# Staging the queries of a slot with one POOL copy in place of four, in a two-part decode attention kernel

## The chip, the cores and the metric

The kernel runs on one core of a Trainium2 chip. The metric is the device time of one execution in microseconds (us). For a program on one core, an execution counts as slow when it lies more than 1.5% above the fastest of the same kernel; all comparisons here use fast runs.

Engines: PE (matrix), DVE (VectorE), ACT (ScalarE), POOL (GpSimd), SP (SyncE, which issues the large loads and the output here). "Span" is the time from the first to the last instruction in the profile. In the profiled execution of the kernel before it is 1.8 us shorter than the device time (244.62 and 246.43 us).

## The reference

Two decode attentions, A and B, with one query token each: 32 query heads of width 128, 16 key/value heads, 8192 cached tokens. A looks at the last 2048 tokens only, B at all.

```python
W = min(4096, max(256, Sk // 4))                  # A: 2048; B: everything
q = (x @ wq) -> 32 heads of 128
scores = einsum("bhqd,bhkd->bhqk", q, k) * Dh ** -0.5
p = softmax(scores); o = einsum("bhqk,bhkd->bhqd", p, v)
return o.reshape(B, Sq, Hq * Dh) @ wo             # A and B concatenated
```

About 103 MB of the inputs are read and the result is 1152 numbers, so the work is mostly reading.

## The kernel before

The work goes in five groups: group 0 is A (16 key/value heads, 2048 tokens each), groups 1 to 4 are B (four heads each, 8192 tokens). SBUF has two key slots (s = 0, 1) and one value region. In each group PE transposes the keys, computes scores against a staged query tile `qst`, and later sums the values. PE runs the five groups as a loop (`Fori`); the other engines' programs are unrolled.

POOL clears tiles at the start and builds identities. After that it does one thing: for each group and slot it copies query columns from `qcol` into the places of `qst` that the scores need.

```python
def q_stage(g, s):
    def go(pool):
        for e in range(2):
            for x in range(2):
                o = s * 514 + e * 260 + x * 128
                if g:
                    dst = bass.AP(tensor=qst, offset=o, ap=[[1024, 128], [40, 4], [1, 2]])
                    src = bass.AP(tensor=qcol, offset=HQ + 8 * (g - 1) + 4 * e + 2 * s,
                                  ap=[[2 * HQ, 128], [0, 4], [1, 2]])
                else:
                    ...                                   # same size, other strides
                ins = pool.tensor_copy(dst, src)
        return ins
    add("pool", go, reads=[("qcol", min(g, 1))], writes=[("qst", s)], tag="q%d" % s)
```

`add` records an operation with what it reads and writes, and later derives the semaphore waits. So a staging waits until the last scores that read the slot's old queries are done, and the next group's scores wait for the staging.

```python
for g in range(NG):                     # the order in which operations are recorded
    for s in range(2): load_k(g, s)
    load_v(g)
    for s in range(2): q_stage(g, s)
    k_transpose(g, 0, 0); k_transpose(g, 1, 1)
    for u in range(2, 8):
        k_scores(g, u - 2, 2 * u)       # u 0..3 read slot 0, u 4..7 slot 1
        k_transpose(g, u, 2 * u + 1)
    ...                                 # scores 6 and 7, softmax, values
...
with self.nc.Block() as block:          # one program for each engine
    @block.gpsimd
    def _(pool): run("pool", pool)
    ...
for P in range(2):                      # after the block: SP waits for the two outputs
    nc.sync.wait_ge(...)
```

## Time and profile before

| | before |
|---|---|
| device time, median of 6 | 246.47 us (246.35 to 246.59) |
| span | 244.6 us |
| load queue, share of 16 DMA engines' span | 98.1% |
| POOL busy | 9.1 us (4%), 57 instructions |

From the page of the kernel before: busy time and share of each engine with its number of instructions, the queue of the loads (packets, MB, share of the DMA engines' span), and the traffic.

```profile
span 244.6 us, 5235 instructions
PE 163.9 (67%) x2325; PEld 119.5 (49%) x2325; DVE 88.2 (36%) x152; ACT 92.5 (38%) x95; POOL 9.1 (4%) x57
...
q1 hardware_dynamic: 3900, 102.76, 98.1%
...
HBM read 102.76 MB, written 0.00 MB: 420 GB/s over the span
```

No engine is busy for more than 67% of the span; the load queue takes 98.1% of the DMA engines' time. From this share I take the kernel to be bound by its reads.

POOL's stagings of the kernel before, from the grouped timeline: start, duration, what, and in brackets how long POOL had been idle and what released it.

```profile
24.17 1.06 POOL L487 COPY qst<-qcol 128x8 bf16<-128x8 bf16 x8 [19.82 <-DVE xpad L447]
48.92 0.56 POOL L487 COPY qst<-qcol 128x8 bf16<-128x8 bf16 x4 [23.68 <-PE sacc L522]
62.63 0.56 POOL L487 COPY qst<-qcol 128x8 bf16<-128x8 bf16 x4 [13.15 <-PE sacc L522]
87.31 0.56 POOL L487 COPY qst<-qcol 128x8 bf16<-128x8 bf16 x4 [24.13 <-PE sacc L522]
95.68 0.56 POOL L487 COPY qst<-qcol 128x8 bf16<-128x8 bf16 x4 [7.81 <-PE sacc L522]
126.11 0.56 POOL L487 COPY qst<-qcol 128x8 bf16<-128x8 bf16 x4 [29.86 <-PE sacc L522]
134.48 0.56 POOL L487 COPY qst<-qcol 128x8 bf16<-128x8 bf16 x4 [7.81 <-PE sacc L522]
165.96 0.56 POOL L487 COPY qst<-qcol 128x8 bf16<-128x8 bf16 x4 [30.93 <-PE sacc L522]
174.33 0.56 POOL L487 COPY qst<-qcol 128x8 bf16<-128x8 bf16 x4 [7.81 <-PE sacc L522]
```

Two scores of group 1 in the kernel before, from PE's timeline: the first that reads slot 0 and the first that reads slot 1.

```profile
78.98 0.64 PE L522 MATMUL sacc<-kt,qst 128*32 128x512 bf16 x8
...
89.06 0.63 PE L522 MATMUL sacc<-kt,qst 128*32 128x512 bf16 x8
```

Read together: slot 1's staging ends at 62.63 + 0.56 = 63.2 us and is first read at 89.1 us, 26 us later. That is the smallest slack of the eight.

### The profile page before, as it was taken

Reading aid. Unit: us, or ns where it says so; the run is one execution under the profiler, and the core shown is the slowest. Engines: PE = TensorE matmul, PEld = TensorE weight load, DVE = VectorE, ACT = ScalarE, POOL = GpSimd, SP = SyncE. Lnnn points to the kernel's source line nnn. Section 1 sums busy time; section 2 is a strip of 40 time slices with the busy share of each in tenths; the row PEclk is TensorE's granted clock in tenths of the full one; section 3 lists DMA queues with packets and bytes.
Section 4 is the critical chain, followed back from the end, with each engine's and each line's share of the span. In section 5 each row is a group of like instructions: output and inputs, shape, how many; then the busy total and the mean of one; then the engine's idle time right before and its main releaser. Section 6 shows DMA issues by size and latency. Waiting matters only on the chain. (4 is left out here: it accounts for less than half of the span.)

```text
span 244.6 us, 5235 instructions
## 1 busy us (share of the span) xinstructions
PE 163.9 (67%) x2325; PEld 119.5 (49%) x2325; DVE 88.2 (36%) x152; ACT 92.5 (38%) x95; POOL 9.1 (4%) x57
## 2 busy tenths in 40 slices
PE   0007339968389995393999162999457799945965
PEld 0002139746236773233866121987232787624854
DVE  0001306854316454204655302455322245543031
ACT  2000016855306786102876300687600378630000
POOL 5000100000000000000000000000000000000000
PEclk9999957997759999569999859799957589975599
DMA  8999999999999999899999999998989999989993
GB/s 313 458 404 419 431 434 426 429 426 431 450 426 430 482 397 461 375 434 429 489 429 429 423 418 429 439 498 386 472 380 429 429 488 397 461 388 422 416 411 137
DMA packets 4068, 102.88 MB, mean 421 GB/s; under 512 B 602, under 2 KB 732, under 8 KB 988
## 3 DMA queue, kind: packets, MB, share of 16 engines
q1 hardware_dynamic: 3900, 102.76, 98.1%
q8 instruction: 6, 0.10, 0.2%
q10 hardware_dynamic: 160, 0.00, 0.0%
q14 instruction: 2, 0.02, 0.0%
HBM read 102.76 MB, written 0.00 MB: 420 GB/s over the span
## 5 line engine op out<-in xcount | busy, mean ns | idle before, releaser
L507 ACT ACTIVATE kt<-ktps 128x1024 bf16<-128x1024 bf16 x80 | 79.3, 1037 | 90.0 <-PE ktps L497 89.9
L497 PE MATMUL ktps<-ident,slots 128*128 128x128 bf16 x1280 | 86.5, 232 | 22.6 <-PEq L214 19.1
L497 PEld LDWEIGHTS ktps<-ident,slots 128*128 128x128 bf16 x1280 | 80.3, 105 | 38.2 <-issue 38.2
L510 DVE COPY kt<-ktps 128x1024 bf16<-128x1024 bf16 x80 | 60.8, 768 | 57.7 <-PE ktps L497 57.6
L589 PE MATMUL opsum<-slots,ptm 128*32 128x512 bf16 x320 | 29.0, 539 | 11.4 <-PEq L214 11.4
L522 PE MATMUL sacc<-kt,qst 128*32 128x512 bf16 x320 | 25.4, 392 | 2.1 <-PEq L214 2.1
L589 PEld LDWEIGHTS opsum<-slots,ptm 128*32 128x32 bf16 x320 | 14.0, 129 | 24.8 <-issue 22.8
L560 PE MATMUL misc<-ident,psb 128*128 128x128 bf16 x40 | 4.4, 276 | 15.8 <-PEq L214 15.8
L607 DVE TENSOR_TENSOR vtmp<-opsum,maskV 128x512 f32<-128x512 f32 x4 | 2.8, 692 | 32.0 <-PE opsum L589 32.0
L548 ACT ACTIVATE psb<-sacc,stat 128x2048 bf16<-128x2048 f32 x5 | 9.8, 1967 | 10.2 <-DVE stat L537 10.2
L560 PEld LDWEIGHTS misc<-ident,psb 128*128 128x128 bf16 x40 | 3.3, 122 | 18.2 <-issue 18.2
L438 PE MATMUL misc<-xnine,twice 64*128 64x18 bf16 x1 | 0.2, 172 | 17.8 <-DMA xnine<-in_B_x_dram 17.8
L487 POOL COPY qst<-qcol 128x8 bf16<-128x8 bf16 x40 | 5.5, 191 | 165.0 <-PE sacc L522 145.2
L567 DVE TENSOR_TENSOR ptm<-misc,maskP 128x1024 bf16<-128x1024 bf16 x5 | 3.5, 692 | 15.8 <-PE misc L560 15.8
L522 PEld LDWEIGHTS sacc<-kt,qst 128*32 128x32 bf16 x320 | 5.0, 94 | 8.3 <-issue 4.8
L438 PEld LDWEIGHTS misc<-xnine,twice 64*128 64x128 bf16 x1 | 0.1, 103 | 17.8 <-issue 17.8
L462 ACT ACTIVATE qrow<-opsum 128x512 bf16<-128x512 f32 x1 | 0.6, 597 | 19.2 <-PE opsum L456 19.2
L691 PE MATMUL ktps<-slots,opj 128*32 128x144 bf16 (+1 forms) x192 | 6.6, 247 | 0.7 <-issue 0.7
L691 PEld LDWEIGHTS ktps<-slots,opj 128*32 128x32 bf16 x192 | 5.3, 96 | 1.8 <-issue 0.9
L447 DVE TENSOR_SCALAR xpad<-misc,par 128x5 bf16<-128x5 f32 (+1 forms) x8 | 1.2, 230 | 13.6 <-PE misc L438 13.6
L535 DVE TENSOR_REDUCE stat<-sacc 128x1 f32<-128x512 f32 x5 | 3.5, 692 | 4.4 <-PE sacc L522 4.4
L560 PE MATMUL turned<-ident,psb 128*128 128x128 bf16 x40 | 4.8, 294 | 0.0
(74 smaller groups left out, 51.5 us busy)
## 6 DMA issues: line engine op xcount, KB each, us to landing
slots<-in_B_k_cache_dram SPq DMA_DIRECT2D x8, 4096.0 KB
slots<-in_A_k_cache_dram SPq DMA_DIRECT2D x4, 2048.0 KB
slots<-in_A_v_cache_dram SPq DMA_DIRECT2D x4, 2048.0 KB
slots<-in_A_wq_dram SPq DMA_DIRECT2D x1, 4608.0 KB, 13.7
slots<-in_B_wq_dram SPq DMA_DIRECT2D x1, 4608.0 KB, 23.8
slots<-in_A_wo_dram SPq DMA_DIRECT2D x1, 4608.0 KB, 18.6
slots<-in_B_wo_dram SPq DMA_DIRECT2D x1, 3024.0 KB, 25.4
slots<-in_B_wo_dram SPq DMA_DIRECT2D x1, 1008.0 KB, 7.6
```

The lines of the kernel that those rows point to most:

```text
L487: ins = pool.tensor_copy(dst, src)
L497: ins = pe.matmul(ktps_bf[q][:, t * 128:(t + 1) * 128], lhsT=slots[:, o:o + 128], rhs=ident[:, :], start=True, stop=True, is_transpose=True)
L507: add("act", lambda act, src=src, dst=dst: act.activation(dst, src, ACT.Copy), reads=[("bank", q)], writes=[("kt", u % NKT, q)], tag="e%d% ...
L510: add("dve", lambda dve, src=src, dst=dst: dve.tensor_copy(dst, src), reads=[("bank", q)], writes=[("kt", u % NKT, q)], tag="e%d%d" % (u, q))
L522: ins = pe.matmul(sacc[32 * j:32 * j + 32, :], lhsT=qst[:, o:o + 32], rhs=rhs, start=(u == 0 and e == 0), stop=True, skip_group_check=True)
L535: add("dve", lambda dve: dve.tensor_reduce(st(C_M + g), sacc[:, :], AX.X, ALU.max), reads=[B_S], writes=[("st", C_M + g)], tag="max")
L548: return act.activation(dst, src, ACT.Exp, bias=st(C_NB + g), scale=SCALE, accum_out=st(C_L + g))
L560: ins = pe.matmul(dst[:, t * 128:(t + 1) * 128], lhsT=psb[:, o:o + 128], rhs=ident[:, :], start=True, stop=True, is_transpose=True)
L567: return dve.tensor_tensor(ptm[:, c * 1024:(c + 1) * 1024].rearrange("p (t y) -> p t y", t=8), dst.rearrange("p (t y) -> p t y", t=8), mas ...
L589: ins = pe.matmul(opsum[64 * j + 32 * x:64 * j + 32 * x + 32, :], lhsT=ptm[:, o:o + 32], rhs=v[:, at[0], at[1], :, :, b:b + 128], start=(n ...
L607: add("dve", lambda dve: dve.tensor_tensor(vtmp[:, :, :], src, by, ALU.mult), reads=[B_O, w], writes=["vtmp"], tag="keep")
L691: ins = pe.matmul(ktps[P][32 * j:32 * j + 32, 0:w], lhsT=opj[:, P, jj:jj + 32], rhs=slots[:, o:o + w], start=(jj == 0), stop=(jj == HQ - 1))
```

## The change

The intent is less work and fewer instructions on POOL. In groups 1 to 4 the four copies have regular offsets (260 for e, 128 for x), so one access pattern with two more dimensions covers them. Group 0 keeps its copies, with the two loops swapped. 40 copies become 16, and POOL's compiled program shrinks from 5,376 to 3,840 bytes.

```diff
     def q_stage(g, s):
         def go(pool):
-            for e in range(2):
-                for x in range(2):
-                    o = s * 514 + e * 260 + x * 128
-                    if g:
-                        dst = bass.AP(tensor=qst, offset=o, ap=[[1024, 128], [40, 4], [1, 2]])
-                        src = bass.AP(tensor=qcol, offset=HQ + 8 * (g - 1) + 4 * e + 2 * s, ap=[[2 * HQ, 128], [0, 4], [1, 2]])
-                    else:
-                        ...
+            if g:
+                dst = bass.AP(tensor=qst, offset=s * 514, ap=[[1024, 128], [260, 2], [128, 2], [40, 4], [1, 2]])
+                src = bass.AP(tensor=qcol, offset=HQ + 8 * (g - 1) + 2 * s, ap=[[2 * HQ, 128], [4, 2], [0, 2], [0, 4], [1, 2]])
+                return pool.tensor_copy(dst, src)
+            for x in range(2):
+                for e in range(2):
+                    ...
                     ins = pool.tensor_copy(dst, src)
             return ins
```

## The prediction

> **What bounds the kernel now.** It streams 102.8 MB into one core, and the stream never stops. The page's queue table gives the load queue 98.1% of 16 DMA engines' span, 420 GB/s over 244.6 us. The windows view, cut at group boundaries, shows a DMA share of 0.97 to 1.04 in every stretch to 213 us; only the output projection's last 32 us fall to 0.84. Busy shares are PE 67%, ACT 38%, DVE 36%, POOL 4%. The chain of waits that ended last holds only PE, DVE and ACT, from 217 us on. The DMA queue's own waits name PE work (scores 82.4, sums 58.6, transposes 24.1 us, and so on) and the output copy; none names POOL.

> **What the change does.** Staging a slot in groups 1 to 4 (eight times in all) becomes one copy of 128x32 instead of four of 128x8. Group 0 keeps its eight copies, in another order: 40 copies become 16. PE's program, the DMAs, the buffers and the semaphore counts stay.

> Cost now: the grouped timeline shows four copies in 0.56 us, 191 ns each with overlap, a new one about every 0.124 us. Cost of the new one, an estimate: POOL's memsets took 104 ns for 8 elements a partition, 204 for 128 and 955 for 1024, about 0.84 ns an element beyond the fixed part; 24 elements more on 191 ns give 0.21 us. [...] I take 0.21 to 0.26 us. All eight save about 2.6 us of POOL; its busy time goes from 9.1 to about 6.4 us.

> **How much of it is critical.** None. Every staging waits for the last scores of its slot, and its reader comes a group later. From the timelines, end of the copies to the first scores that read them: slot 0 49.5 to 79.0, 87.9 to 117.5, 126.7 to 157.9, 166.5 to 197.8 us; slot 1 63.2 to 89.1, 96.2 to 127.9, 135.0 to 167.7, 174.9 to 207.6 us. The least is 26 us. Group 0's, untouched, has 15.6 us. The line view lists nobody that waited for the copies. Even a new copy ten times as slow would stay hidden.

> Side effects. [...] The trace shows no cost of it: the score maximum beside the staging at 62.6 us took 0.69 us like the other four. Twenty-four instructions fewer to fetch is too little beside 102.8 MB.

> **Prediction.** 246.5 us, unchanged; range 245.8 to 247.2, only scatter between builds and chips. Faster by over 2%: 0.01; within 2%: 0.98; slower by over 2%: 0.01.

> **What would show each step.** Right: 16 staging instructions, eight of 128x32 at 0.2 to 0.3 us, POOL busy about 6.4 us; the load queue still at 98%; group starts (transposes at 75.0 us, last scores at 213.5) within 0.3 us of before. Wrong: a copy of many us; a PE wait on the staging; DMA issues at other times.

> **What would make it wrong.** A new shape that POOL runs by a very slow path (over 26 us); a shift of the loads' timing at which the DMA engines run at another rate (slices of the page range from 375 to 498 GB/s); another chip with another clock or memory rate.

The lower end of the new copy's cost, 0.21 us, comes from the memsets; the upper end, 0.26 us, was an allowance of mine that no measurement here shows. With both ends the sum was eight times 0.56 less 0.21 to 0.26 us, which is 2.4 to 2.8 us less work on POOL, put at 2.6, and nothing of it on the device time. The second gave a reason for which POOL could slow VectorE; "no cost of it" speaks of that slowing. "Fetch" is my word for what the page shows as packets on two instruction queues (q8 and q14 in the kernel before: 0.10 and 0.02 MB).

## More of the kernel before

The end of `Block` is a barrier. As the trace records it, every engine reports to a semaphore, POOL waits for all of them, and POOL then releases all the others. In the kernel before, the other four report at 222.38, 242.60, 242.94 and 244.01 us, POOL's wait is over at 244.04, and the four go on at 244.52 to 244.53, after POOL's release at 244.48.

## The result, and the profile after

| | before | after |
|---|---|---|
| device time, median of 6 | 246.47 us (246.35 to 246.59) | 246.08 us (245.87 to 246.14) |
| span of the profiled run | 244.6 us | 244.6 us |
| POOL busy | 9.1 us | 6.3 us |

The ratio is 0.9984, with a 95% interval of 0.9971 to 0.9996. A ratio is the mean time of one kernel's fast runs over that of the other's of the same rounds, so it is not quite the ratio of the medians. The slowest run after (246.14) is faster than the fastest before (246.35), so a difference of 0.39 us is there to be explained.

The answering lines of the page after:

```profile
span 244.6 us, 5211 instructions
PE 165.4 (68%) x2325; PEld 121.3 (50%) x2325; DVE 88.2 (36%) x152; ACT 92.7 (38%) x95; POOL 6.3 (3%) x33
...
q1 hardware_dynamic: 3900, 102.76, 98.1%
...
HBM read 102.76 MB, written 0.00 MB: 420 GB/s over the span
```

POOL's stagings after, from the grouped timeline:

```profile
24.37 1.06 POOL L486 COPY qst<-qcol 128x8 bf16<-128x8 bf16 x8 [20.02 <-DVE xpad L447]
48.95 0.21 POOL L481 COPY qst<-qcol 128x32 bf16<-128x32 bf16 x1 [23.51 <-PE sacc L521]
62.62 0.21 POOL L481 COPY qst<-qcol 128x32 bf16<-128x32 bf16 x1 [13.47 <-PE sacc L521]
87.34 0.21 POOL L481 COPY qst<-qcol 128x32 bf16<-128x32 bf16 x1 [24.50 <-PE sacc L521]
95.71 0.21 POOL L481 COPY qst<-qcol 128x32 bf16<-128x32 bf16 x1 [8.16 <-PE sacc L521]
127.20 0.21 POOL L481 COPY qst<-qcol 128x32 bf16<-128x32 bf16 x1 [31.28 <-PE sacc L521]
135.56 0.21 POOL L481 COPY qst<-qcol 128x32 bf16<-128x32 bf16 x1 [8.16 <-PE sacc L521]
165.97 0.21 POOL L481 COPY qst<-qcol 128x32 bf16<-128x32 bf16 x1 [30.19 <-PE sacc L521]
174.34 0.21 POOL L481 COPY qst<-qcol 128x32 bf16<-128x32 bf16 x1 [8.16 <-PE sacc L521]
```

The new copy takes 0.21 us as estimated, and the load queue's share is the same. Six of the eight merged stagings start within 0.03 us of before. The two of group 3 start 1.1 us later. That is scatter and not the change: the first of them starts anywhere from 126.1 to 128.6 us in the traces without fills, at 128.3 in a run that has all 40 copies (before_pad2 below). The groups themselves start where they did (group 1's transposes at 75.04 us, before 75.01; the last scores at 213.71, before 213.78). The span, too, is the same, so nothing in it accounts for 0.39 us.

So the gain must lie in the way the program ends. The profile's views do not count semaphore instructions, but the trace holds them. These are the last records of POOL and SP in both kernels (us from the start of the span):

```
before                                             after
243.538  SP    drain starts; SP reports 0.47 later 243.554
244.036  POOL  has waited for all engines          244.051
244.475  POOL  releases all engines                244.129
244.517  SP    sees the release                    244.171
244.593  SP    has waited for the outputs to land  244.559
245.16   an 8192-byte instruction packet           none
```

Before the change POOL takes 0.439 us between "all are there" and "go on"; after it takes 0.078 us. The other four engines stand still meanwhile: their next records come 0.042 to 0.054 us after the release, in both kernels. The span doesn't show it, because SP's very last instruction waits for the output to land, which happens at 244.54 us in both kernels, after the release. In the kernel before, a packet of 8192 bytes on an instruction queue starts 0.54 us after the end of the last instruction (244.62 us). In the kernel after there is none.

### The profile page after: what moved, and what is told of

Same layout as the page of the kernel before. It is cut to its first block, busy times and chain, and to the rows that moved or that the text cites. A ratio compares the mean times of both kernels' runs of the same rounds, so it can differ in the third digit from the quotient of the medians.

```text
span 244.6 us, 5211 instructions
## 1 busy us (share of the span) xinstructions
PE 165.4 (68%) x2325; PEld 121.3 (50%) x2325; DVE 88.2 (36%) x152; ACT 92.7 (38%) x95; POOL 6.3 (3%) x33
## 3 DMA queue, kind: packets, MB, share of 16 engines
q1 hardware_dynamic: 3900, 102.76, 98.1%
## 5 line engine op out<-in xcount | busy, mean ns | idle before, releaser
L496 PE MATMUL ktps<-ident,slots 128*128 128x128 bf16 x1280 | 87.8, 234 | 22.5 <-PEq L214 19.2
L496 PEld LDWEIGHTS ktps<-ident,slots 128*128 128x128 bf16 x1280 | 81.7, 106 | 38.0 <-issue 37.9
L588 PE MATMUL opsum<-slots,ptm 128*32 128x512 bf16 x320 | 28.5, 532 | 9.8 <-PEq L214 9.8
L447 DVE TENSOR_SCALAR xpad<-misc,par 128x5 bf16<-128x5 f32 (+1 forms) x8 | 1.2, 229 | 13.8 <-PE misc L438 13.8
L481 POOL COPY qst<-qcol 128x32 bf16<-128x32 bf16 x8 | 1.7, 211 | 147.4 <-PE sacc L521 147.4
L559 PE MATMUL turned<-ident,psb 128*128 128x128 bf16 x40 | 5.3, 313 | 0.0
## 6 DMA issues: line engine op xcount, KB each, us to landing
slots<-in_A_wq_dram SPq DMA_DIRECT2D x1, 4608.0 KB, 13.8
```

The lines of the kernel that those rows point to most:

```text
L496: ins = pe.matmul(ktps_bf[q][:, t * 128:(t + 1) * 128], lhsT=slots[:, o:o + 128], rhs=ident[:, :], start=True, stop=True, is_transpose=True)
L559: ins = pe.matmul(dst[:, t * 128:(t + 1) * 128], lhsT=psb[:, o:o + 128], rhs=ident[:, :], start=True, stop=True, is_transpose=True)
L588: ins = pe.matmul(opsum[64 * j + 32 * x:64 * j + 32 * x + 32, :], lhsT=ptm[:, o:o + 32], rhs=v[:, at[0], at[1], :, :, b:b + 128], start=(n ...
```

## The experiments

All kernels below gave correct results. Each ran in 5 rounds, heavy32k in one. A "pad" is a semaphore instruction: it adds or subtracts one on a semaphore that nobody reads. It adds nothing to POOL's busy time (6.29 us with 24 pads, 6.28 in the kernel after). Pads stand at the end of the engine's program, ahead of the closing barrier:

```diff
+    spare = nc.alloc_semaphore("spare")
+    for k in range(24):                      # or another number
+        add("pool", lambda e, k=k: e.sem_inc(spare, (1, -1)[k % 2]))
     prog.emit()
```

On POOL a pad takes 0.078 to 0.084 us (in pad88), at about 175 us, when POOL has finished its stagings and would otherwise wait for 69 us. Runs of one set share a chip and the runs of the kernel before. The three sets ran on three different chips.

### Set 1: is it the copies, or the length of the program?

Theory F in the expectations was a guess: the time goes with the late 8192-byte instruction packet, which they call a fetch.

**after_again**: the changed kernel, unaltered.

> The changed kernel once more, unaltered, as the control of this chip. The gain on record is 0.39 us (246.47 to 246.08), while the span from first to last instruction is 244.6 us in both. Theory F (fetch at the end): [...] so 246.1 us, 0.3 to 0.5 below the kernel before, no such packet, span unchanged at 244.6. Rival W (POOL's work): the gain comes from 2.7 us less work on POOL; also 246.1. Rival S (scatter between builds and chips): any difference from -0.5 to +0.5 us.

Measured: 246.01 us against 246.37 for before, ratio 0.9985 (0.9972 to 0.9999). The gain repeats. One of its five runs, the profiled one, took 246.39 us, as long as before. Its trace has neither the pause nor the late packet; its span is longer (244.8 us, the other four 244.4 to 244.6).

**pad24**: the changed kernel with 24 pads on POOL.

> The changed kernel, with 24 instructions of POOL's sequencer alone (adding and subtracting one on a semaphore nobody reads) after its last staging, so that its program is as long as before while its copies stay merged. Theory F: the time goes back to 246.5 us (0.3 to 0.5 above the changed kernel), the trace again has an 8192-byte instruction fetch after the last instruction, the span stays at 244.6 us. Rival W: 246.1 us, as POOL's copies are as in the changed kernel. Rival S: no relation to length.

Measured: 246.40 us, ratio 1.0001 (0.9987 to 1.0015). The gain is gone, although the copies are merged as before. POOL's two closing instructions are 0.435 us apart again, and the late packet is back at 245.14 us. This rules out the rival that the gain is saved copy work.

**pad88**: the same with 88 pads.

> The same with 88 such instructions, so that POOL's program is 64 instructions longer than before the change. If length itself costs, the time is 246.5 us or more. Theory F in its sharper form, [...] the time is 246.1 us although the program is the longest. Rival W: 246.1 us too, with no fetch moved.

The reason for the 246.1 us was my guess: what counts is a place in the program, which 88 pads would bring to about 175 us, where POOL still has 69 us to wait.

Measured: 245.93 us, ratio 0.9984 (0.9971 to 0.9998). The longest program is as fast as the shortest. The records of POOL show where the pause went:

```
pad 26 of 88   176.187 us
pad 27         176.622      0.435 us later; every other pad follows the one before by 0.078 to 0.084
```

The packet starts after the pause in every trace that shows both: 0.7 us after it in the kernel before, nearly 4 us after it here. So the packet goes with the pause, and the time of the packet is not the time of the pause. My expectation named the fetch itself as the cost; that part was not shown. I went on with the sharper form: a pause at a place in the stream.

**sp_pad34**: 34 pads on SP instead.

> The changed kernel with 34 such instructions at the end of SyncE's program (its compiled program then is as long as POOL's before the change, 84 instructions), POOL's left short. Theory F[...]: a late fetch comes back on another engine and the time is 246.5 us; since SyncE waits for the output's landing last, its 34 instructions come before that wait and add nothing by themselves. If only POOL's fetch counts: 246.1 us. Rival W: 246.1 us. Rival S: no relation.

Measured: 247.48 us, ratio 1.0050 (1.0036 to 1.0064); the expectation was wrong. No late packet appeared and POOL's closers were 0.078 us apart. The pads ran one after the other from 243.32 to 245.29 us and held back SP's report to the barrier, which came at 245.36 us. In after_again it came at 244.28 us. I had thought that the wait for the output's landing would hide them, but the execution ends about 2 us after POOL's release (1.92 us here, 1.96 in before, 2.01 in after; device time less the place of the release in the span), wherever the landing is: here at 244.33 us, before the release at 245.46. So this run does not tell whether another engine has such a place. It does show that delay ahead of the barrier reaches the device time.

### Set 2: a fixed place, tested by moving the program past it

**before_pad2**: the kernel *before*, all 40 copies, with two pads more.

> The kernel before, all 40 copies kept, with two idle sequencer instructions more at the end of POOL's program. The first four runs show a pause of 0.435 us in place of 0.078 at one fixed place of POOL's instruction stream: between its two instructions that close the final barrier in the kernel before and with 24 pads, and 64 instructions further up, at 176.6 us, with 88 pads. Theory P (a place in the stream, sharper than F: what counts is whether the pause falls between POOL's wait for all engines and its release of them): two instructions more push the two closers past the place, the pause falls at about 175 us where POOL has 69 us to wait, and the time drops to 246.0 us, 0.3 to 0.5 below the kernel before, with a longer program and no copy merged; the closers are 0.08 us apart. Rival W (copies' work) and rival L (program length): 246.4 us or more. Rival S (scatter): 246.4.

Measured: 246.00 us against 246.41 for before, ratio 0.9983 (0.9969 to 0.9997). The whole gain of the change arrives with none of its copies merged and with a longer program. The closers are 0.084 us apart, and the packet comes at 179.44 us instead of 245.16. The pause itself cannot be told apart here, among copies that are still running.

**pad23**: the changed kernel with 23 pads.

> The changed kernel with 23 pads, one fewer than the 24 that gave 246.4 us. Theory P: the place now lies just behind POOL's release; the other engines are let go in time, closers 0.08 us apart. If what follows the release on POOL is not what ends the execution, 246.0 us; if POOL's own closing part is, 246.4 still. Rival L: 246.4, as 24.

Measured: 246.39 us, ratio 1.0002 (0.9988 to 1.0016). The closers are 0.079 us apart, so the other engines were released in time. Yet the late packet is there (245.10 us), and the execution ended 2.38 us after the release in place of 1.9 to 2.0. The trace's semaphore records show the delay behind the release: the last update of the barrier's semaphores, which follows the last instruction in every trace, comes 1.63 us after the release here, against 1.14 to 1.17 us in all runs without a late packet and 1.21 in before and pad24. So with the place just behind POOL's release, the closing part is late by about 0.5 us (1.63 less 1.14 to 1.17), and the end of the execution by 0.4 to 0.5 us. On which engine the delay lies was not shown.

**pad12**: 12 pads.

> The changed kernel with 12 pads. Theory P: as with 23, the place lies behind the release, if it is crossed at all before POOL stops; closers 0.08 us apart, 246.0 us. A rival in which the cost grows with length: halfway, 246.2 us.

Measured: 245.98 us, ratio 0.9980 (0.9966 to 0.9993), closers 0.078 us apart, no late packet.

**heavy16k**: the changed kernel, where each merged staging first fills a scratch tile on POOL.

```diff
+    lag = nc.alloc_sbuf_tensor("lag", [128, 16384], mybir.dt.uint8)
...
+        if g:
+            add("pool", lambda pool: pool.memset(lag[:, :], 0), reads=["lag"], writes=["lag", ("qst", s)])
             # and the copy also reads "lag", so that it waits for the fill
```

> The changed kernel, where each of the eight merged stagings first fills a scratch tile of 128x16384 bytes that nobody reads, on POOL, and the copy waits for it: by 0.84 ns an element about 13.8 us more in each staging (an estimate from the memsets of before), 110 us of POOL in all, 8 program entries more. The slack read from the trace is 26 us for the tightest slot, and two stagings in a row fit while one takes under about 20 us (48.9 + 2x20 = 89 us, when the first group-1 score of slot 1 reads). Theory H (staging is hidden): 246.0 us, as the changed kernel, no PE wait on staging. Rival W: slower by some us. If fills contend with VectorE's copies on the way into SBUF, those beside it get longer than 0.69 us.

Measured: 245.94 us, ratio 0.9984 (0.9970 to 0.9997). From the group view of its POOL instructions (count, busy us and mean ns, idle time before them and who ended it):

```profile
L491 POOL MEMSET lag<- 128x16384 uint8 x8 | 110.0, 13752 | 55.6 <-PE sacc L528 55.6
L482 POOL COPY qst<-qcol 128x32 bf16<-128x32 bf16 x8 | 1.7, 212 | 0.5
```

110 us of extra POOL work cost nothing. Removing 2.7 us could then hardly gain anything. The eight fills leave POOL's program 16 instructions shorter than before, between after and pad12 on the scale below, so its end is a fast one too. VectorE's 80 key copies took 772 ns on average in this run, against 768 in the changed kernel; the median is 692 ns both beside the fills (31 copies) and away from them. So these copies were not visibly disturbed. Other VectorE instructions beside the fills were not looked at.

### Set 3: a step or a slope, and a control for the slack

**pad26**: 26 pads.

> The changed kernel with 26 pads, two more than the 24 that gave 246.4 us. Theory P: the two closers now lie behind the place, the pause falls where POOL waits from 175 us on; 246.0 us, closers 0.08 us apart. Rival L (length): 246.4 us or more.

Measured: 246.13 us against 246.52 on this chip, ratio 0.9982 (0.9968 to 0.9997). Closers 0.083 us apart, packet at 180.55 us. The pause is in the trace where the theory puts it, two instructions ahead of the release: POOL's drain, the instruction between the last pad and the closing wait, starts 0.434 us after that pad, at 176.95 us; in pad24 it starts 0.081 us after it. One of the nine runs of before in this set took 786 us; it counts as slow and is left out.

**pad18**: 18 pads.

> The changed kernel with 18 pads; 12 gave 246.0 us and 23 gave 246.4. Theory P says a step and not a slope: either 246.0 or 246.4 us, with a fetch after the last instruction if and only if it is 246.4. A cost that grows with length would give 246.2 us.

Measured: 246.13 us, ratio 0.9983 (0.9969 to 0.9997), no late packet. It is a step and not a slope. Its profiled execution alone took 246.37 us and ended 2.16 us after the release, without a late packet. The last update of the barrier's semaphores comes 1.14 us after the release, as in pad12, so this delay lies later than the one in pad23. The end of one execution scatters that much, so single times decide little here.

**heavy32k**: as heavy16k, with two fills for each staging.

> The changed kernel with two fills of 13.75 us in each merged staging, 27.7 us for one. Beyond the limit of about 20 us that the slack gave. Theory H: POOL becomes the chain, stagings follow each other without idle from 47.8 us: the eight end at 75.5, 103.2, 130.9, 158.6, 186.3, 214.0, 241.7 and 269.4 us, the last scores end near 276 us in place of 214, and the whole takes about 306 us (range 300 to 312), with PE waits on the staging in the profile. If the slack were not what hides the staging, the time would stay at 246 or the 13.75 us of the run before would have shown.

Measured: 310.07 us (two executions of one round, 309.73 and 310.42), span 308.7. The stagings now follow each other without idle time, and the last ends at 270.8 us (expected 269.4). Its timeline, POOL and then PE:

```profile
76.42 27.56 POOL L491 MEMSET lag<- 128x16384 uint8 x2
104.04 0.21 POOL L482 COPY qst<-qcol 128x32 bf16<-128x32 bf16 x1
...
104.39 1.05 PE L528 MATMUL sacc<-kt,qst 128*32 128x512 bf16 x8 [15.48 <-PEq L214]
```

The fifth score of group 1 starts 0.14 us after its staging ends (104.04 + 0.21 = 104.25), having idled 15.48 us. The slack was real, and it has an end. One trap is visible here: the wait is on POOL's copy, but the bracket names PE's own sequencer, PEq. The list of PE's waits in this run does the same:

```profile
PE sacc L528 <- PEq L214: 79.2, 12, 17.9
```

In the kernel before, the same line is small:

```profile
PE sacc L522 <- PEq L214: 2.1, 5, 0.7
```

So "nobody waited for POOL" could not be read from the names of the releasers. It could be read from start and end times, and from this sum.

### All pad runs on one scale

| run | POOL program against before | gap between closers, us | 8192-byte packet near the end | device time, us | before on that chip, us |
|---|---|---|---|---|---|
| after (again) | 24 shorter | 0.078 | none | 246.01 | 246.37 |
| pad12 | 12 shorter | 0.078 | none | 245.98 | 246.41 |
| pad18 | 6 shorter | 0.078 | none | 246.13 | 246.52 |
| pad23 | 1 shorter | 0.079 | 245.10 us | 246.39 | 246.41 |
| pad24 | equal | 0.435 | 245.14 us | 246.40 | 246.37 |
| before_pad2 | 2 longer | 0.084 | 179.44 us | 246.00 | 246.41 |
| pad26 | 2 longer | 0.083 | 180.55 us | 246.13 | 246.52 |
| pad88 | 64 longer | 0.079 | 180.49 us | 245.93 | 246.37 |

The slow lengths are "equal" and "1 shorter". Of the lengths that were run, those shorter by 6 or more and those longer by 2 or more are fast; 2 to 5 shorter and 1 longer were not run.

## Why the prediction was right or wrong

**The time and the class: right.** 246.08 us lies in the range of 245.8 to 247.2, and the result is within 2%. The range was wide enough for scatter; it was not drawn for the effect that moved the time, so that 246.08 falls in it is partly luck.

**POOL's stagings are off the critical path: right, and shown.** heavy16k adds 110 us to POOL at no cost. heavy32k goes past the slack that the timelines gave and costs 64 us, close to what that slack foretold (about 306 us expected, 310.07 measured). That the reads are the bound is in keeping with a load queue at 98.1% before and after, but no run tests it.

**The new copy's cost: right.** 0.211 us against 0.21 to 0.26. The 24 further elements a partition took 20 ns (211 against 191 ns), as the estimate from the memsets had it; the upper end had no measurement behind it. POOL's busy time is 6.3 us against 6.4.

**"Even a new copy ten times as slow would stay hidden": right.** heavy16k made a staging over 60 times as slow (13.96 against 0.21 us).

**"The line view lists nobody that waited for the copies": true, but poor evidence.** In heavy32k PE waits for the copies and the view still names PEq. The slack from the timelines carried the argument.

**"The trace shows no cost of it", of POOL slowing VectorE: true of what was looked at, but little evidence.** The prediction looked at one instruction, a score maximum that reads a tile in PSUM (0.69 us, like the other four); heavy16k adds the key copies, which read from PSUM as well (median 692 ns beside the fills and away from them).

**"246.5 us, unchanged ... only scatter", and "Twenty-four instructions fewer to fetch is too little beside 102.8 MB": wrong in size.** The term was set to zero and measured 0.39 us. I had weighed the instructions as bytes on the DMA queues (1,536 bytes). What their number moved is a pause at one place of POOL's stream. POOL is the engine that releases the closing barrier, and the old length put that place exactly between its wait and its release. The pause makes 0.439 - 0.078 = 0.36 us of the 0.39 us between the medians; the rest is within the scatter of single executions. The step that failed is thus "only scatter": the prediction looked at the copies and their readers, and not at the barrier that ends the program, where all engines go on only after POOL's release (0.042 to 0.054 us after it). pad24, before_pad2 and pad26 show that the position of the program decides it, and neither the copies nor the length as such.

**Open.** What the pause consists of is not shown. In the kernel before POOL sits 69 us in the closing wait (174.89 to 244.04 us) and the pause of 0.439 us still comes behind it. In pad24, pad26 and pad88 it lies at the same place of the stream, and in each of them an 8192-byte instruction packet goes with it. But the packet always starts after the pause, and no trace records a wait for instructions by name. The trace's queue label also does not say whose packet it is; that it is POOL's rests on its moving with the length of POOL's program.

## What to carry to other kernels

When a change to an idle engine moves the device time by a few tenths of a us and the span not at all, look at the closing barrier in the trace's semaphore records before crediting the change: a pad of two idle instructions gave this kernel the same gain as the merged copies (0.41 us in before_pad2, 0.36 in after_again). Test such small gains with programs of other lengths: here the gain belonged to a position, and 24 further instructions took it away again (pad24, 246.40 us). Read an engine's slack from start and end times, and prove it with a deliberate delay on each side of the limit.
